# Banded attention and a gated two-layer product on one core: other landing times and due times for the planner that writes the order

## The chip, the cores and the metric

The kernel runs on one core of one Trainium2 chip. The metric is the device time of one execution in microseconds, lower is better. The engines are TensorE (PE, with its weight loads as PEld), VectorE (DVE), ScalarE (ACT), GpSimd (POOL) and SyncE (SP), which issues nearly all transfers in one queue, in order.

## What is computed

```python
scores = scale * np.matmul(q, k.transpose(0, 1, 3, 2))      # 8 batches, 8 heads, 576 x 64
mask = (rel >= 0) & (rel < window)                          # window = 64
scores = np.where(mask, scores, -1000000000.0)
scores = scores - np.max(scores, axis=-1, keepdims=True)
attn = np.exp(scores)
attn = attn / (np.sum(attn, axis=-1, keepdims=True) + 1e-09)
attn_out = np.matmul(attn, v)
x = attn_out.transpose(0, 2, 1, 3).reshape(B * S, H * D)    # 4608 x 512
h = x @ w_in                                                # 512 -> 2048
g = np.where(h >= 1, h, np.where(h <= -1, 0.0, (h + 1) ** 2 / 4))
return g @ w_out                                            # 2048 -> 512
```

All of it is in float32. Each query sees the 64 keys up to itself.

## The kernel before

**Two kinds of work.** The 4608 tokens are 36 attention steps of 128 queries and all 8 heads. Their results feed the two-layer product. The first 1536 tokens are three plain tiles of 512. For each of them PE multiplies 16 pieces of the hidden layer (`ffn_in`, L1118), ScalarE, VectorE and GpSimd make the gate (L1128 to L1150), and PE multiplies by the second matrix (`ffn_out`, L1164). The other 3072 tokens are three supers of 1024 tokens. In a super each matrix product is cut into 2 x 2 blocks and done with seven block products in place of eight, out of sums of blocks. So a super has two halves of 56 products each: L893 (`ffn_product`) and L979 (`out_product`), six matmuls of 128 x 512 to a product, since each float32 operand is split into a high and a low part and three of the four cross terms are taken. The results are added up on VectorE (L908, L998), the gate is on L1128 to L1140, and the operands of the second half are prepared by L957 (sums of blocks), L273 (high part) and L970 (low part). The sums of the blocks of the weights are made once, from the second plain tile on (`add_sums`, L814 to L834), and kept in DRAM (`kept`). From there every product of a super loads its 256 KB (`ring_load`, L873) into one of seven buffers, in turn.

**An attention step.** PE makes the scores (L422, 32 instructions and 64 records of the trace), VectorE adds the mask (L443) and takes the maximum (L452, L453), ScalarE takes the exponential (L464, 16 pieces), VectorE inverts the sum (L475, L476), VectorE or GpSimd normalises (L483), and PE multiplies by V (L534, 16 instructions, 32 records). Before the product with V the weights have to be transposed. Steps 0 to 7 do this on PE or VectorE. Steps from `SOON` = 8 on do it through DRAM: VectorE transposes blocks of 32 x 32 (`att_turn`, L490), SyncE writes the result in two transfers (`att_write`, L501, 192 KB each) to `moved` and reads it back in another shape (`att_read`, L504, 512 KB) into `ptd`, of which there is one buffer for this (called `turned`). The read waits until both writes have landed and until the values of the step before are done; the values wait until the read has landed. I call this way from L490 to L534 the hop. The steps of a super are done in the order 0, 4, 1, 5, 2, 6, 3, 7 during the super before it, and the values become the operands of the next super (L569, L605). Steps 12 to 19 feed the first super, 20 to 27 the second, 28 to 35 the third.

**What sets the order.** A planner (class `Plan`) writes the whole program. Each piece of work has a key, a cost on each engine that may do it, what it needs, the buffers that it takes and gives back, and a lag from the end of its cost to the moment when others may use it. For a transfer the cost is the issue on SyncE and the lag is the landing. The planner goes through time: at each engine, of the pieces that could begin first (within `PATIENCE`), it takes the one with the lowest key. It does this with the constants at the head of the file, and the program then runs in that order, whatever the chip's own times are. An engine that comes to a piece whose input isn't there stands still, with all that is behind it. Keys in turn are due times: `a_keys` for the scores of a step, `B_DUE` for what follows, `R_LEAD` ahead of a product for its ring load, `S_LATE` for the sums of the weights, `OP_LEAD` and `D_LEAD` for the operands, `G_LEAD` for the gates, `BUILD` for the operands of the next super.

Of the kernel before, what the change touches and what calls it, by code (L numbers as in the profile page):

```python
# [40 lines left out]
W_LEAD = 0.57  # L41
W_FIRST = (20.54, -1.96, 1.46, 0.57, -0.16)
W_STEP = 4 / 3
L_LEAD = 2
W_LATE = (3.88, 0.0, -0.24, 7.77, 11.92, 15.5, 19.73)
W_LOAD = 1400
Q_LOAD = 700
# [23 lines left out]
EXP = 1545, 1440  # L71
S_PE = 1230, 1070
B_PE = 2050
B_DUE = 1.0, 2.5, 0.5
B_STEP = 16 / 3
B_FIRST = 3.44
A_END = 1.5
V_PE = 1270
# [1 line left out]
G_LATE = (2.37, 0.0, 0.23, -4.22, 1.33)  # L80
D_LATE = (0.0, 0.0, 2.51, -4.53, 0.66, 1.46)
TURN = 965, 1500
HOP_SP = 600
HOP_LAG = 2300, 2800
PATIENCE = dict(ACT=300, DVE=0, Pool=303, PE=0, SP=0)
BUFS = dict(qt=2, kt=2, vt=4, ps_a=2, sm=2, ptd=3, pt2=1, x=2, u=2, ps_h=2, a=2, gh=2, gl=2, acc=4, o=2, tmp=2)
BUFS.update({n: 1 for n in ("xtmp", "xs0", "xs1", "xs2", "xs3", "xs4", "xs5", "X", "Y")}, raw=4, ring=7, op=5)
# [2 lines left out]
PLAIN = 3  # L90
SUPERS = 3
H_STEP = 18.67
S_LATE = 0
S_PACE = 1.8
O_CHANGE = 3.33, 3.2, 4.7
EARLY_2 = 1.5
A_SUPER = (5, 3.3), (9, 3.6)
A_ORDER = (0, 4, 1, 5, 2, 6, 3, 7)
BUILD = -12, 2
X_SLOTS = 4, 0, 6, 1, 2, 3  # L100
G_FIRST = 8
RING_SLOT = 7
PARTS = (0, 0, 0), (1, 1, 1), (0, 5, 4), (1, 3, 2), (0, 4, 3), (1, 6, 5), (0, 2, 6)
WRITES = (1, None), (2, 1), (0, None), (3, 2), (3, 3), (1, 2), (2, 2)
R_LEAD = 3
R_LOAD = 400
L_DVE = 4, 6, 8
G_LEAD = 0, 0, 0, 0
OP_LEAD = 2.5
D_LEAD = 1.0  # L110


class Plan:
# [10 lines left out]
    def add(self, key, cost, do, after=(), takes=(), gives=(), lag=0, shared=False):  # L124
        self.work.append((key, cost, do, set(after), takes, gives, lag, shared))
        return len(self.work) - 1
# [75 lines left out]
def banded_attention_then_ffn(ctx: ExitStack, tc: tile.TileContext, q, k, v, w, masks, out, out_t, dims):  # L202
# [185 lines left out]
    def load_q(s):  # L388
        qts[s] = t = ld.tile([P, NP, SB], F32, name="qt", bufs=BUFS["qt"])
        nc.sync.dma_start(out=t, in_=q[s])  # L390

    def load_k(s, eng=nc.sync):
        kts[s] = t = ld.tile([P, NP, 3 * QB], F32, name="kt", bufs=BUFS["kt"])
        eng.dma_start(out=t, in_=k[s])
# [255 lines left out]
    def add_step(t, i):  # L650
# [16 lines left out]
            last["r"] = add(lk, dict(ACT=480), lambda e: round_masks())  # L667
        if s == PE_STEPS - 2:
            last["m"] = add(lk + M_LATE, dict(SP=590), lambda e: load_masks(), lag=DMA_LAG)
        xq = add(lk, dict(SP=Q_LOAD), lambda e: load_q(s), takes=["qt"], lag=DMA_LAG)  # L670
        xk = add(lk, dict(SP=K_LOAD), lambda e: load_k(s) if s else None, takes=["kt"], lag=DMA_LAG)
        xv = add(lk + V_LATE, dict(SP=Q_LOAD), lambda e: load_v(s, 0), last["v"], takes=["vt"], lag=DMA_LAG)
        xw = add(lk + V_LATE, dict(SP=Q_LOAD), lambda e: load_v(s, 1), [xv], takes=["vt"], lag=DMA_LAG)
        last["v"] = [xw]
        needs = [xq, xk] + [last["r"]] * masked + last["s"]
        if before:
# [18 lines left out]
        if s < SOON:  # L695
            for h in range(2):
                x = xs
                if not masked:
                    x = add(due + D_LATE[0], dict(DVE=MASKED[near(s)]), lambda e, h=h: att_masked(s, h), [x, last["m"]] if near(s) else [x], gives=[(ps, xs, h)])
                x = add(due + D_LATE[1], dict(DVE=800 if masked else MAXIMUM[near(s)]), lambda e, h=h: att_max(s, h, masked), [x])  # L700
                x = add(
                    due + D_LATE[2], dict(ACT=1375 if masked else EXP[near(s)]), lambda e, h=h: att_exp(s, h, masked), [x],
                    gives=[(ps, xs, h)] * masked,
                )
                x = add(due + D_LATE[3], dict(DVE=420), lambda e, h=h: att_inverse(s, h), [x])
                x = add(due + D_LATE[4], NORM[1], lambda e, h=h: att_normalize(s, h, e), [x], shared=True)
                if not near(s):
                    xt_ = add(
                        key, dict(PE=440), lambda e, h=h: att_transpose_pe(s, h, pt), [x] + turned, takes=[pt],
                        gives=[("sm", xs)] * h,  # L710
                    )
                    turned = [xt_]
                    x = add(
                        due + D_LATE[5], dict(ACT=485, DVE=608), lambda e, h=h: att_transposed(s, h, e), [xt_] + first,
                        takes=["ptd"], gives=[(pt, xt_)],
                    )
                    first = [x]
                    taken.append(x)
                else:
                    x = add(  # L720
                        due, dict(DVE=1890), lambda e, h=h: att_transpose(s, h, 0), [x] + first, takes=["ptd"]
                    )
                    first = [x]
                    taken.append(x)
                    x = add(due, dict(DVE=1890), lambda e, h=h: att_transpose(s, h, 1), [x] + ready, gives=[("sm", xs)] * h)
                ready.append(x)
            gives = [("ptd", taken[0]), ("ptd", taken[1])]
        else:
            due = [key + B_DUE[0], key + B_DUE[0] + B_DUE[2]]
            x = [add(due[h], dict(DVE=MASKED[1]), lambda e, h=h: att_masked(s, h), [xs, last["m"]], gives=[(ps, xs, h)]) for h in range(2)]  # L730
            x = add(due[0], dict(DVE=930), lambda e: att_max(s, BOTH, False), x)
            x = [add(due[h], dict(ACT=EXP[1]), lambda e, h=h: att_exp(s, h, False), [x]) for h in range(2)]
            x = add(due[1], dict(DVE=430), lambda e: att_inverse(s, BOTH), x)
            x = [add(due[1], dict(DVE=870, Pool=1650), lambda e: att_normalize(s, BOTH, e), [x], shared=True)]
            due = key + B_DUE[1]
            if s == SOON:
                z = add(due - 2, dict(Pool=600), lambda e: att_clear(), early_values)
                last["d"] = [add(due - 2, dict(SP=HOP_SP), lambda e, j=j: att_zero(j), [z], lag=HOP_LAG[0]) for j in range(2)]
            x = add(due, dict(DVE=TURN[0]), lambda e: att_turn(s), x, lag=TURN[1])
            x = [add(due, dict(SP=HOP_SP), lambda e, j=j: att_write(s, j), [x, *last["d"]], lag=HOP_LAG[0], gives=[("sm", xs)] * j) for j in range(2)]  # L740
            x = add(due, dict(SP=HOP_SP), lambda e: att_read(), x + last["t"], takes=["pt2"], lag=HOP_LAG[1])
            first = taken = ready = last["d"] = [x]
            gives = [("pt2", taken[0])]
        last["t"] = first
# [93 lines left out]
    def add_sums(l, n):  # L838
        key = step(1) + S_PACE * (n + l * NF // 2) + S_LATE
        ready = [w_ready[2 * n, l], w_ready[2 * n + 1, l], w_ready[NF - 1, 0], w_ready[NF - 1, 1]]  # L840
        xp = add(key, dict(SP=2000), lambda e: sum_pass(l, n), ready, lag=O_LAG_DMA)
        reads, keeps = [xp], [xp]
        for c in range(2):
            k = key + c * S_PACE / 2
            xs = add(
                k, tt(2 * P), lambda e, c=c: sum_whole(l, n, c, 0, e), ready + sum_last,
                takes=["tmp"] if sum_first else ["tmp", "u"], shared=True,
            )
            if not sum_first:
                sum_first.append(xs)  # L850
            x0 = add(k, tt(2 * P), lambda e, c=c: sum_whole(l, n, c, 1, e), [xs], shared=True)
            reads.append(x0)
            sum_last[:] = [xs]
            x = x0
            for j in range(4):
                x = add(k, tt(P), lambda e, c=c, j=j: sum_sums(l, n, c, j, e), [x], shared=True)
            xh = add(k, dict(ACT=90 + .84 * 4 * P), lambda e, c=c: sum_high(l, n, c, e), [x], takes=["o"])
            x = add(k, tt(4 * P), lambda e, c=c: sum_low(l, n, c, e), [xh], shared=True)
            x = add(k, dict(SP=750), lambda e, c=c: sum_keep(l, n, c), [x], lag=O_LAG_DMA, gives=[("tmp", xs), ("o", xh)])
            keeps.append(x)  # L860
        sums_read[l, n], sums_kept[l, n] = reads, keeps

# [12 lines left out]
    def add_ring(l, u, n, j, key):  # L875
        after = [*sums_kept[l, n], *ring_last]
        if l == 0 and u == 0 and n == 0:
            after += freed([RING_SLOT]) + [gates_end[0]] + early_values
        x = add(key - R_LEAD, dict(SP=R_LOAD), lambda e: ring_load(l, u, n, j, x), after, takes=["ring"], lag=DMA_LAG)
        if not ring_last:  # L880
            ring_last.append(x)
        return x
# [127 lines left out]
    def add_outs(u, gates):  # L1010
# [23 lines left out]
        for j in range(7):  # L1034
# [61 lines left out]
            if end:  # L1096
                for m in range(2):
                    gives = []
                    if m:
                        gives = [(("X", box_x) if j == 6 else ("Y", box_y))]  # L1100
                        if j == 5:
                            gives += [("o", o_box, 0), ("o", o_box, 1)]
                    st = add(
                        at, dict(SP=500), lambda e, j=j, m=m, to=to, box=box: out_store(u, to, box, m), [some[m], *([st] if m else [])],
                        lag=O_LAG_DMA, gives=gives,
                    )

    highs = {}
# [283 lines left out]
```

## Time and profile before

| | |
|---|---|
| median of three runs | 905.01 us (902.1 to 910.52) |
| the profiled execution | 911.83 us, its span 909.9 us |
| granted TensorE clock, mean | 0.974 |
| PE busy | 846.9 us, 93% of the span |
| VectorE, ScalarE, GpSimd busy | 712.2, 531.5 and 239.4 us |
| moved by DMA | 213.28 MB, 234 GB/s |

All durations are of the one profiled execution. A row of waits names who waited for whom, the sum, how often and the longest. A row of a group of instructions has its count, then busy time and the mean of one in ns, then the idle time before them and what ended it. In rows of transfers the last number is the median from issue to landing, in us. Names of lines are those of the kernel before; in the changed kernel the same lines stand 8 further down, and from L674 on 10.

### The profile page before, as it was taken

How to read it: one execution, taken by the hardware profiler on the slowest of the kernel's cores; microseconds unless marked ns; L12 is line 12 of the kernel's file. 1: busy time of each engine (PE TensorE's matmuls, PEld its weight loads, DVE VectorE, ACT ScalarE, POOL GpSimd, SP SyncE). 2: the span in 40 equal slices, each digit the busy share in tenths (PEclk: the TensorE clock that was granted, in tenths of full speed). 3: DMA queues.
4: the chain of work that ended last, by engine and by line, in shares of the span. 5: the costliest groups of instructions: out<-in, count | busy, mean ns of one | idle time of the engine just before them, and what ended most of it. 6: DMA issues, size and time to landing. Idle time of an engine off the chain costs nothing.

```text
span 909.9 us, 18124 instructions
## 1 busy us (share of the span) xinstructions
PE 846.9 (93%) x6540; PEld 685.4 (75%) x6540; DVE 712.2 (78%) x1256; ACT 531.5 (58%) x1296; POOL 239.4 (26%) x252
## 2 busy tenths in 40 slices
PE   7899999899998999799988998979988989999998
PEld 6788887678776777678776777868777778888886
DVE  6999995579877774568878974888888965878874
ACT  6999965456654464546665552655764534556442
POOL 1000055447543543111134320222334211110100
PEclk9999999899999999799999999999999999999999
DMA  8991189977987554877877887878876777666775
GB/s 320 418 377 54 40 260 349 369 222 214 274 269 207 161 161 133 271 223 226 259 226 231 277 260 247 246 252 241 284 244 214 230 235 214 194 195 194 191 223 168
DMA packets 149832, 213.28 MB, mean 234 GB/s; under 512 B 11760, under 2 KB 73968, under 8 KB 149744
## 3 DMA queue, kind: packets, MB, share of 16 engines
q1 hardware_dynamic: 149456, 211.22, 74.2%
q8 instruction: 52, 0.85, 0.4%
q10 hardware_dynamic: 288, 0.92, 0.3%
q14 instruction: 36, 0.29, 0.1%
HBM read 162.15 MB, written 49.94 MB: 233 GB/s over the span
## 4 chain that ended last, share of the span: by engine, by line
PE 39%; DMA 16%; DVE 10%; ACT 3%; issue 1%; SPq 1%; POOL 0%; ACTq 0%; POOLq 0%; DVEq 0%
PE acc L979 16%; PE ps_h L893 8%; PE acc L893 8%; DMA ptd<-moved 7%; DMA moved<-sm 5%; PE ps_a L534 3%; PE acc L1164 2%; PE ps_h L1118 2%; DMA kept<-u 1%; DMA wts<-kept 1%; DVE op L970 1%; DVE g L957 1%; ACT sm L464 1%; DVE sm L490 1%; DVE g L1140 1%
## 5 line engine op out<-in xcount | busy, mean ns | idle before, releaser
L979 PE MATMUL acc<-op,wts 128*128 128x512 f32 x576 | 143.5, 401 | 0.0
L1118 PE MATMUL ps_h<-xh,wts 128*128 128x512 f32 (+1 forms) x424 | 134.7, 384 | 7.6 <-DVE a L1140 5.2
L979 PEld LDWEIGHTS acc<-op,wts 128*128 128x128 f32 x576 | 110.9, 194 | 24.2
L273 ACT CAST op<-g 128x512 fp32r<-128x512 f32 x118 | 73.4, 622 | 89.1 <-PE acc L979 68.2
L1164 PE MATMUL acc<-wts,gh 128*128 128x512 f32 x384 | 121.1, 396 | 0.0
L970 DVE TENSOR_TENSOR op<-g,op 128x512 fp32r<-128x512 f32 x105 | 78.0, 744 | 30.0 <-ACT op L273 29.5
L893 PE MATMUL ps_h<-wts 128*128 128x512 f32 x360 | 96.4, 405 | 3.1 <-DMA wts<-kept 3.1
L1118 PEld LDWEIGHTS ps_h<-xh,wts 128*128 128x128 f32 x424 | 79.9, 195 | 25.2 <-DVE a L1140 6.8
L893 PE MATMUL acc<-wts 128*128 128x512 f32 x360 | 94.2, 398 | 0.7 <-DMA wts<-kept 0.7
L464 ACT ACTIVATE sm<-sm,nm 128x96 f32<-128x96 f32 x224 | 80.8, 362 | 19.0 <-DVE nm L453 18.9
L1133 ACT ACTIVATE a<-a 128x512 f32<-128x512 f32 (+1 forms) x139 | 85.7, 617 | 4.3
L1128 ACT ACTIVATE a<-g 128x512 f32<-128x512 f32 x96 | 60.4, 629 | 42.9 <-DVE g L908 38.2
L970 POOL TENSOR_TENSOR op<-g,op 128x512 fp32r<-128x512 f32 x30 | 41.8, 1397 | 159.8 <-DVE op L275 101.3
L893 PEld LDWEIGHTS ps_h<-wts 128*128 128x128 f32 x360 | 69.0, 194 | 18.7 <-issue 3.3
L1164 PEld LDWEIGHTS acc<-wts,gh 128*128 128x128 f32 x384 | 70.7, 189 | 15.3 <-issue 0.3
L1118 PE MATMUL ps_h<-xl,wts 128*128 128x512 f32 (+1 forms) x212 | 80.5, 380 | 0.9 <-DVE xl L547 0.9
L893 PEld LDWEIGHTS acc<-wts 128*128 128x128 f32 x360 | 68.8, 192 | 16.3 <-DMA wts<-kept 1.4
L534 PE MATMUL ps_a<-ptd,vt 128*64 128x64 f32 x992 | 38.1, 233 | 41.2 <-DMA ptd<-moved 26.3
L1164 PE MATMUL acc<-wts,gl 128*128 128x512 f32 x192 | 75.2, 392 | 0.0
L534 PEld LDWEIGHTS ps_a<-ptd,vt 128*64 128x64 f32 x992 | 34.1, 145 | 52.7 <-issue 19.5
L1140 DVE SCALAR_TENSOR_TENSOR g<-a,g 128x512 f32<-128x512 f32 x96 | 67.8, 709 | 3.3 <-ACT a L1133 3.2
L957 POOL TENSOR_TENSOR g<-g 128x512 f32<-128x512 f32 x22 | 31.4, 1430 | 147.1 <-DVE op L970 53.1
(146 smaller groups left out, 1625.4 us busy)
## 6 DMA issues: line engine op xcount, KB each, us to landing
wts<-kept SPq DMA_DIRECT2D x240, 256.0 KB, 3.3
vt<-in_v SPq DMA_DIRECT2D x72, 256.0 KB, 3.7
ptd<-moved SPq DMA_DIRECT2D x28, 512.0 KB, 4.9
kt<-in_k SPq DMA_DIRECT2D x35, 384.0 KB, 5.1
kept<-wts SPq DMA_DIRECT2D x48, 256.0 KB, 4.8
gh<-kept SPq DMA_DIRECT2D x48, 256.0 KB, 3.1
gl<-kept SPq DMA_DIRECT2D x48, 256.0 KB, 3.2
raw<-in_w SPq DMA_DIRECT2D x12, 1023.8 KB, 11.1
```

The lines of the kernel that those rows point to most:

```text
L273: nc.scalar.copy(dst, src)
L464: nc.scalar.activation(t, t, AF.Exp, bias=nm[:, g:g + 1], scale=scale, accum_out=den[:, g:g + 1])
L534: nc.tensor.matmul(ps[half[h], p, n], lhsT=vt[i][:, c:c + D], rhs=w_, start=True, stop=True)
L893: nc.tensor.matmul(ps, lhsT=r[:, part, cp], rhs=x_op(k, xp)[:, cp], start=j in (0, 1, 3, 4) and i == 0 and cp == 0, stop=j in (1, 2, 5, 6) ...
L957: engine[eng].tensor_tensor(out=g[:, out], in0=g[:, a], in1=g[:, b], op=op)
L970: engine[eng].tensor_tensor(out=low, in0=g_of(n)[:, of], in1=high.bitcast(F32), op=ALU.subtract)
L979: nc.tensor.matmul(opened[b][m], lhsT=r[:, part, m], rhs=op[xp], start=j in (0, 1, 3, 4) and i == 0 and n == 0, stop=j in (1, 2, 5, 6) and ...
L1118: nc.tensor.matmul(ps, lhsT=wts[f, 0][:, part, c * P:(c + 1) * P], rhs=x[:, c, r], start=(c == 0 and j == 0), stop=(c == NP - 1 and j == 2),)
L1128: nc.scalar.activation(gs[t, f, r.start][0], phs[t, f, r.start], AF.Relu, bias=0.5, scale=0.5)
L1133: nc.scalar.activation(a, a, AF.Square)
L1140: nc.vector.scalar_tensor_tensor(out=ps if t >= PLAIN else a, in0=a, scalar=1.0, in1=ps, op0=ALU.min, op1=ALU.max)
L1164: nc.tensor.matmul(acc[t, i][:, n], lhsT=g[:, sub], rhs=wts[f, 1][:, part, n], start=(q == 0 and j == 0), stop=(q == NF - 1 and j == 2 and ...
```

## The change

No instruction is added or taken away. The planner gets other numbers. The transfers of the later stage get landing times of their own: for the hop 2900 ns (write) and 4500 ns (read) in place of 2300 and 2800, with an issue cost of 690 and 460 in place of 600; for ring loads, K, Q and V of steps from 8 on 2900, 4500, 3500 and 3100 in place of 1300; for stores of results and of weight sums 3500 in place of 2300, with 1150 in place of 750 to issue a pair of the latter. Loads of V of these steps are due nearly with those of K and Q (`V_LATE_2`), no longer 6.28 later. And the due times and leads of the later stage are other numbers.

```diff
-L_LEAD = 2
+L_LEAD = 2.31
...
-B_DUE = 1.0, 2.5, 0.5
-B_STEP = 16 / 3
+B_DUE = (1.0, 2.34, -0.14)
+B_STEP = 5.21
...
-HOP_SP = 600
-HOP_LAG = 2300, 2800
+HOP_SP = 690, 460
+HOP_LAG = 2900, 4500
+RING_LAG = 2900
+K_LAG = 4500
+Q_LAG = 3500
+V_LAG = 3100
+STORE_LAG = 3500
+SUM_PASS = 1950
+SUM_KEEP = 1150
+V_LATE_2 = 0.15
...
-S_LATE = 0
+S_LATE = 3.55
...
-A_SUPER = (5, 3.3), (9, 3.6)
+A_SUPER = ((5.16, 3.3), (8.9, 3.34))
...
-BUILD = -12, 2
+BUILD = (-14.15, 3.64)
...
-R_LEAD = 3
-R_LOAD = 400
+R_LEAD = 3.76
+R_LOAD = 430
...
-G_LEAD = 0, 0, 0, 0
-OP_LEAD = 2.5
-D_LEAD = 1.0
+G_LEAD = (1.7, 0, 0, 0.54)
+OP_LEAD = 2.0
+D_LEAD = 0.76
...
-        xq = add(lk, dict(SP=Q_LOAD), lambda e: load_q(s), takes=["qt"], lag=DMA_LAG)
-        xk = add(lk, dict(SP=K_LOAD), lambda e: load_k(s) if s else None, takes=["kt"], lag=DMA_LAG)
-        xv = add(lk + V_LATE, dict(SP=Q_LOAD), lambda e: load_v(s, 0), last["v"], takes=["vt"], lag=DMA_LAG)
-        xw = add(lk + V_LATE, dict(SP=Q_LOAD), lambda e: load_v(s, 1), [xv], takes=["vt"], lag=DMA_LAG)
+        late = s >= SOON
+        xq = add(lk, dict(SP=Q_LOAD), lambda e: load_q(s), takes=["qt"], lag=Q_LAG if late else DMA_LAG)
+        xk = add(lk, dict(SP=Q_LOAD if late else K_LOAD), lambda e: load_k(s) if s else None, takes=["kt"], lag=K_LAG if late else DMA_LAG)
+        vk, vl = lk + (V_LATE_2 if late else V_LATE), V_LAG if late else DMA_LAG
+        xv = add(vk, dict(SP=Q_LOAD), lambda e: load_v(s, 0), last["v"], takes=["vt"], lag=vl)
+        xw = add(vk, dict(SP=Q_LOAD), lambda e: load_v(s, 1), [xv], takes=["vt"], lag=vl)
...
-                last["d"] = [add(due - 2, dict(SP=HOP_SP), lambda e, j=j: att_zero(j), [z], lag=HOP_LAG[0]) for j in range(2)]
+                last["d"] = [add(due - 2, dict(SP=HOP_SP[0]), lambda e, j=j: att_zero(j), [z], lag=HOP_LAG[0]) for j in range(2)]
...
-            x = [add(due, dict(SP=HOP_SP), lambda e, j=j: att_write(s, j), [x, *last["d"]], lag=HOP_LAG[0], gives=[("sm", xs)] * j) for j in range(2)]
-            x = add(due, dict(SP=HOP_SP), lambda e: att_read(), x + last["t"], takes=["pt2"], lag=HOP_LAG[1])
+            x = [add(due, dict(SP=HOP_SP[0]), lambda e, j=j: att_write(s, j), [x, *last["d"]], lag=HOP_LAG[0], gives=[("sm", xs)] * j) for j in range(2)]
+            x = add(due, dict(SP=HOP_SP[1]), lambda e: att_read(), x + last["t"], takes=["pt2"], lag=HOP_LAG[1])
...
-        xp = add(key, dict(SP=2000), lambda e: sum_pass(l, n), ready, lag=O_LAG_DMA)
+        xp = add(key, dict(SP=SUM_PASS), lambda e: sum_pass(l, n), ready, lag=O_LAG_DMA)
...
-            x = add(k, dict(SP=750), lambda e, c=c: sum_keep(l, n, c), [x], lag=O_LAG_DMA, gives=[("tmp", xs), ("o", xh)])
+            x = add(k, dict(SP=SUM_KEEP), lambda e, c=c: sum_keep(l, n, c), [x], lag=STORE_LAG, gives=[("tmp", xs), ("o", xh)])
...
-        x = add(key - R_LEAD, dict(SP=R_LOAD), lambda e: ring_load(l, u, n, j, x), after, takes=["ring"], lag=DMA_LAG)
+        x = add(key - R_LEAD, dict(SP=R_LOAD), lambda e: ring_load(l, u, n, j, x), after, takes=["ring"], lag=RING_LAG)
...
-                        lag=O_LAG_DMA, gives=gives,
+                        lag=STORE_LAG, gives=gives,
```

The order is the same until shortly before the values of step 8. From there on all engines have another order. Three places are shown.

SyncE, the hop of step 34 in the second super: two writes (L501), the read (L504), and ring loads (L873). Before:

```order
L873 DMA wts<-kept_106 128x512
L873 DMA wts<-kept_107 128x512
L501 DMA moved<-sm 64x3x256
L873 DMA wts<-kept_108 128x512
L501 DMA moved<-sm 64x3x256
L873 DMA wts<-kept_101 128x512
L873 DMA wts<-kept_102 128x512
L504 DMA ptd<-moved 128x2x512
```

And with the change, where the lines are L509, L512 and L883, and L408 is a load of V:

```order
L509 DMA moved<-sm 64x3x256
L883 DMA wts<-kept_102 128x512
L509 DMA moved<-sm 64x3x256
L883 DMA gh<-kept_103 128x512
L408 DMA vt<-in_v 128x1x512
L883 DMA gl<-kept_104 128x512
L512 DMA ptd<-moved 128x2x512
```

Between the second write and the read stand two ring loads, as before, and now a load of V too.

PE, the values of the same step (the last row), and the products (L979) ahead of them; a product is one row of x6, or five rows where it has its operand in gh and gl; L422 are the scores of step 31. Before:

```order
L979 MATMUL acc<-gh,wts 128x512
L979 MATMUL acc<-gl,wts 128x512
L979 MATMUL acc<-gh,wts 128x512 x2
L979 MATMUL acc<-gl,wts 128x512
L979 MATMUL acc<-gh,wts 128x512
L422 MATMUL ps_a<-kt,qt 32x96 x32
L979 MATMUL acc<-op,gh 128x512 x6
L979 MATMUL acc<-op,gl 128x512 x6
L979 MATMUL acc<-op,wts 128x512 x6
L534 MATMUL ps_a<-ptd,vt 64x64 x16
```

With the change (L989, L430 and L542):

```order
L989 MATMUL acc<-op,gh 128x512 x6
L430 MATMUL ps_a<-kt,qt 32x96 x32
L989 MATMUL acc<-op,gl 128x512 x6
L989 MATMUL acc<-op,wts 128x512 x12
L989 MATMUL acc<-gh,wts 128x512
L989 MATMUL acc<-gl,wts 128x512
L989 MATMUL acc<-gh,wts 128x512 x2
L989 MATMUL acc<-gl,wts 128x512
L989 MATMUL acc<-gh,wts 128x512
L989 MATMUL acc<-op,wts 128x512 x12
L542 MATMUL ps_a<-ptd,vt 64x64 x16
```

Between the scores of step 31 and the values of step 34 stood three products, and now stand six.

PE, the entry to the first super: the last product of the plain tiles (L1164), scores of steps 20 and 24 (L422), and the first products of the super (L893). Before:

```order
L422 MATMUL ps_a<-kt,qt 32x96 x32
L1164 MATMUL acc<-wts,gh 128x512 x2
L1164 MATMUL acc<-wts,gl 128x512
L1164 MATMUL acc<-wts,gh 128x512 x2
L1164 MATMUL acc<-wts,gl 128x512
L422 MATMUL ps_a<-kt,qt 32x96 x32
L893 MATMUL ps_h<-wts 128x512 x6
L893 MATMUL acc<-wts 128x512 x6
```

With the change the rows begin with the values of step 19 (L542), and L430 x64 are the scores of steps 24 and 21:

```order
L542 MATMUL ps_a<-ptd,vt 64x64 x16
L1174 MATMUL acc<-wts,gh 128x512 x2
L1174 MATMUL acc<-wts,gl 128x512
L1174 MATMUL acc<-wts,gh 128x512 x2
L1174 MATMUL acc<-wts,gl 128x512
L1174 MATMUL acc<-wts,gh 128x512 x2
L1174 MATMUL acc<-wts,gl 128x512
L430 MATMUL ps_a<-kt,qt 32x96 x64
L903 MATMUL ps_h<-wts 128x512 x6
L542 MATMUL ps_a<-ptd,vt 64x64 x16
L903 MATMUL acc<-wts 128x512 x6
```

The scores of step 21 have moved ahead of the first product, and the values of step 20 (L542) stand behind the first product, where they stood behind the tenth.

## The prediction

> **What bounds the kernel now.** I read the busy times first, then the kernel cut into stages, then who waited inside each stage, and last the chain of work that ended last.
>
> ```profile
> PE 846.9 (93%) x6540; PEld 685.4 (75%) x6540; DVE 712.2 (78%) x1256; ACT 531.5 (58%) x1296; POOL 239.4 (26%) x252
> PE 39%; DMA 16%; DVE 10%; ACT 3%; issue 1%; SPq 1%; POOL 0%; ACTq 0%; POOLq 0%; DVEq 0%
> ```
>
> TensorE (PE) is busy for 93% of the span, so all that any new order can win is the idle 63 us and what the clock loses. In the chain transfers come second: work on PE alternates with a wait for DMA. The stages show where (columns: sum, busy of PE, PEld, DVE, ACT, POOL, granted clock, DMA share, GB/s):
>
> ```profile
> 165.00:355.00 190.00, 177.34 (x1609) 141.12 (x1609) 140.44 (x261) 105.30 (x306) 91.76 (x104) 0.97 0.73 221
> 355.00:395.00 40.00, 32.88 (x289) 24.97 (x288) 22.83 (x41) 19.37 (x57) 9.58 (x9) 0.83 0.76 240
> 395.00:563.00 168.00, 155.59 (x1203) 125.83 (x1202) 137.85 (x227) 93.28 (x229) 44.83 (x36) 0.97 0.80 246
> 563.00:754.00 191.00, 176.04 (x1442) 142.00 (x1441) 155.30 (x259) 107.45 (x274) 52.67 (x42) 0.98 0.78 242
> 754.00:910.00 156.00, 152.30 (x672) 125.80 (x671) 114.55 (x179) 76.72 (x124) 11.65 (x9) 1.00 0.69 197
> ```
>
> The last stage, the third super, has no attention left and runs at full clock without idle time but for its tail. The first two supers idle 12.4 us (168 - 155.6) and 15.0 us (191 - 176.0) after 395. One group of instructions accounts for nearly all of it:
>
> ```profile
> L534 PE MATMUL ps_a<-ptd,vt 128*64 128x64 f32 x480 | 18.7, 235 | 27.4 <-DMA ptd<-moved 22.3 <-DVE op L275 2.4 <-DVE g L908 1.8
> ```
>
> These are the value products of 15 attention steps (480 matmuls, 32 each) between 395 and 754. PE stood idle for 27.4 us before them, 1.8 us each, for the weights that come back from DRAM (the few us under DVE names are instructions long done; the transfer was last there too). One such hop in the chain, at the end of the first super (start, length, what):
>
> ```profile
> 540.35 0.62 SPq L501
> 541.02 4.90 DMA moved<-sm
> 545.94 5.91 DMA ptd<-moved
> 551.99 1.26 PE ps_a L534 x32
> 553.26 9.83 PE acc L979 x36
> 563.09 1.36 PE ps_h L893 x6
> ```
>
> SyncE issues the write (L501), 4.9 us later it has landed, the read follows at once and takes 5.9 us, and only then does PE go on. The 36 matmuls behind it took 9.83 us. The same 36 took 8.40 us elsewhere, and the granted clock tells why:
>
> ```profile
> 716.97 8.40 PE acc L979 x36
> 460.00:470.00 10.00, 7.30 (x53) 5.84 (x52) 5.50 (x10) 5.29 (x16) 1.79 (x2) 0.83 0.70 239
> 740.00:750.00 10.00, 7.49 (x54) 5.89 (x53) 5.85 (x14) 3.26 (x7) 0.00 (x0) 0.83 0.66 224
> ```
>
> Behind five of the waits (464, 488, 552, 679 and 744 us) the clock is at half for some 3.4 us; 0.83 over 10 us is a loss of 1.7 us each, 8.5 us in all.
>
> **The change, part by part.** No instruction is added or removed. Every term is a wait that another order shortens or makes.
>
> *Value products of the supers (395 to 754).* The planner reckoned with 2300 ns to land the write and 2800 ns for the read. It now reckons with 2900 and 4500. The trace has (between 395 and 754 the count, size and median from issue to landing; in the last row the ns of an issue, shortest, median and longest):
>
> ```profile
> wts<-kept SPq DMA_DIRECT2D x150, 256.0 KB, 3.6
> ptd<-moved SPq DMA_DIRECT2D x14, 512.0 KB, 5.1
> moved<-sm SPq DMA_DIRECT2D x28, 192.0 KB, 4.0
> L873 SPq DMA_DIRECT2D wts<-kept x240: 319/320/1349, 360.7 to 894.1; - x120
> ```
>
> The new figures, with the issue (0.69 and 0.46 us), make 3.6 and 5.0 us against medians of 4.0 and 5.1; the old ones made 2.9 and 3.4. What it does to the order can be counted. SyncE issues in order, and a ring load ahead of the read waits until PE has done the product that held its buffer, seven loads earlier. At ten of the 15 steps that product stood 3 products ahead of the values, at four of them 4; now it is 5 at twelve, 4 at one, and more at the other two. For the last ring load ahead of the second write it was 5 to 7 at all but one and is now 7 or 8, or more. A product is 1.36 us (L893 x6 above). The read's way from that release: load issue 0.32, read 5.1, start of PE and gaps 0.2, some 5.7 us, against 3 x 1.36 = 4.1 us before and 6.8 us now. The write's way: 0.3 + 0.6 + 4.0 + 5.1 + 0.2 = 10.2 us against 6.8 us before and 9.5 us now. So both gain 2 products, 2.7 us, over a mean wait of 1.8 us. What stays is the write's 0.7 us at some steps, nothing at others, and landings longer than the median: I take 0.5 us each, 7.5 us. At the last step of the second super the values move the other way, 17 products behind the scores where it was 20, but the transposition on VectorE (L490) now stands 16 rows behind the masks where it was 28. I count it like the others. **Gain 27.4 - 7.5 = 20 us**, between 5 (if landings lengthen, see the rivals) and 27.
>
> *The clock.* With waits of some 0.5 us I take two thirds of 8.5 us back, **6 us**, between 0 and 8.5. The granted clock fell behind waits of 3.5 us at most:
>
> ```profile
> PE ps_a L534 <- DMA ptd<-moved: 22.3, 11, 3.5
> ```
>
> [...]
>
> *The plain tiles (165 to 355).* PE idles 12.7 us here (190 - 177.3), and 0.97 of 190 us is another 5.7 us of clock.
>
> ```profile
> PE ps_a L534 <- DVE u L821: 5.3, 2, 4.4
> PE ps_h L1118 <- DVE a L1140: 4.3, 3, 3.7
> DVE u L814 <- DMA kept<-u: 15.1, 10, 5.4
> ```
>
> VectorE stands 15.1 us at the head of its queue for the store of the weight sums (L834), whose buffer the next sum (L814) needs, and a gate (L1140) is queued behind it that PE waits for. The planner reckoned with 2.3 us of landing for these stores and 0.75 us of issue, and now with 3.5 and 1.15. These sums also start later (S_LATE 3.55). The eleven hops here get 2.3 us more, as those of the supers. I take half of 18.4, **9 us**, between 0 (SyncE has the same stores to issue either way, and later ones fall among the hops) and 15.
>
> *Entry to the first super (355 to 395).* PE idles 7.1 us, and 0.83 of 40 us is 6.8 us of clock.
>
> ```profile
> PE ps_h L893 <- DMA wts<-kept: 3.1, 1, 3.1
> PE ps_a L534 <- DMA ptd<-moved: 2.9, 1, 2.9
> ```
>
> The first ring load may only go when the last plain product is done. The new order puts the scores of two steps into that gap, where one stood, but the second write of step 20 now stands behind this ring load, and its values come after one product where ten stood. From the last plain product: 0.3 + 0.6 + 4.0 + 5.1 = 10 us to the values, with 3.5 us of work in between (two scores at 1.07, one product), so 6.5 us idle and as much clock lost as now. **0 us**, between -4 and +3.
>
> *Moved at no price.* Loads of V, K and Q change places on SyncE. They are off the path as long as they land before the scores, and no wait for vt, kt or qt of PE stands in these stages. The third super has no waits to win.
>
> Sum: 20 + 6 + 9 + 0 = 35 us. The profiled execution took 911.83 us (span 909.9 and 1.9 around it), so 876.8; the runs shown have a median of 905.01, 0.75% less, and by the same share this is **870 us**.
>
> **The rivals.**
>
> *Landings lengthen with the load, and half of the gain goes.* The same transfers in the plain stage:
>
> ```profile
> ptd<-moved SPq DMA_DIRECT2D x11, 512.0 KB, 4.4
> moved<-sm SPq DMA_DIRECT2D x22, 192.0 KB, 3.0
> ```
>
> At a DMA share of 0.73 write and read make 7.4 us, at 0.79 they make 9.1. The same bytes in 20 us less make a share of some 0.84, by that slope 1.4 us more per hop. Of the 2.7 us half is left: waits of 1.2 us (18 us), a third of the clock term (3), 5 of the plain stage: 9.4 + 3 + 5 = 17, so 888 us. For it speaks the slope; against it, that the step from 0.73 to 0.79 also brings other transfers, not only more. [...]
>
> *The change does not do what it says: VectorE takes the place of the transfers.* It is busy 137.9 of 168 us and 155.3 of 191. In 20 us less that is 0.87 or so, and what is queued on it (transposition, gates, operands) comes late as often as the hops did. PE would wait the 27 us for operands, and only the plain stage gains a little: 900 us. Against it: operands (L970) never show among PE's waits now, and VectorE itself idles 66 us in these stages.
>
> *Slower: a load of V ahead of a write or a read.* These wait longest on SyncE for their buffers (us in total, times, longest):
>
> ```profile
> SPq L873 <- PE acc L979: 79.0, 85, 5.4
> SPq L400 <- PE ps_a L534: 31.3, 12, 5.0
> ```
>
> In the new order such a load stands between a step's first write and its read at seven of the 15 steps, before at two. Should each hold its hop for 8 us, of which 2.7 are covered, that is 7 x 5.3 = 37 us of new waits and 7 x 1.7 = 12 of clock, against 23 us won elsewhere (8/15 of 26, and 9): 26 us more than now, 931 us. It decides from a hold of 5.6 us on (7 x 2.9 + 12 - 23 = 9 us). Against it: the buffer is freed by the values of an earlier step, and so is the buffer that the read itself needs (one `turned`), seven or more products earlier.
>
> **How the numbers follow.** The forecast, 856 to 883, gets 0.62; the longer landings (883 to 898) 0.20; VectorE 0.12; slower 0.06. Of the longer landings I count 0.18 below 896 and put 0.04 of the chance that VectorE leaves some gain there too. The smallest change that a measurement can tell here is 1%, some 9 us. Faster by more: 0.62 + 0.18 + 0.04 = 0.84. Within 1%: 0.10. Slower: 0.06. The range runs from 856 (all 54 us of waits and clock in the first two supers and plain tiles but 5 gone) to 896.
>
> **What would show it.** In the new profile the idle time before the value products of the supers (L542 there) should be near 8 us in place of 27.4, the share of DMA in the chain below a tenth, and the two supers some 13 us shorter each, with a clock of 0.99 after the entry. The wait of VectorE on `kept<-u` should fall by half. The entry keeps its 7 us. Wrong would be: waits of over 1 us left at most value products with landings over 10 us (first rival), idle time before the products (L989, L903 there) in their place (second), or SyncE's waits at the loads of V doubled (third).

## The result and the profile after

The changed kernel takes 866.85 us (median of four runs, 865.92 to 869.91) against 903.56 us before (four runs, 901.72 to 910.52): a ratio of 0.959, interval 0.953 to 0.964. The forecast was 870 us. The profiled execution took 867.29 us.

First the busy times and the chain of the new profile's page:

```profile
PE 829.1 (96%) x6540; PEld 670.8 (78%) x6540; DVE 711.8 (82%) x1254; ACT 530.8 (61%) x1300; POOL 245.9 (28%) x250
PE 67%; DMA 13%; DVE 12%; ACT 3%; issue 2%; SPq 1%; POOL 1%; DVEq 0%; ACTq 0%; POOLq 0%
```

PE has the same 6540 matmuls and is busy 17.8 us less: that is the half clock that is gone (mean granted clock 0.996, before 0.974). VectorE, ScalarE and GpSimd share 2804 instructions as before, with a few of them on another engine. The chain now runs along PE for two thirds of the span; transfers still have 13% of it. The stages, cut where the work is the same as in the windows shown of before (columns: sum, busy of PE, PEld, DVE, ACT, POOL, granted clock, DMA share, GB/s):

```profile
165.00:350.00 185.00, 176.95 (x1711) 140.72 (x1710) 140.60 (x276) 106.93 (x322) 94.51 (x106) 1.00 0.78 236
350.00:390.00 40.00, 34.42 (x284) 27.52 (x284) 28.32 (x48) 22.26 (x62) 9.34 (x9) 0.91 0.90 288
390.00:542.00 152.00, 148.28 (x1132) 120.00 (x1131) 131.88 (x214) 86.31 (x209) 42.26 (x32) 1.00 0.83 261
542.00:716.00 174.00, 172.55 (x1439) 138.72 (x1438) 157.10 (x251) 106.19 (x275) 65.06 (x48) 1.00 0.84 264
716.00:866.00 150.00, 145.77 (x644) 120.40 (x642) 113.65 (x173) 78.75 (x127) 7.77 (x6) 1.00 0.68 196
```

The two supers idle 3.7 us (152 - 148.3) and 1.5 us (174 - 172.6), where it was 12.4 and 15.0, and the granted clock is full there (1.00 in both rows). VectorE is now busy 90% of the second one. The value products of the same 15 steps, between 390 and 716:

```profile
L542 PE MATMUL ps_a<-ptd,vt 128*64 128x64 f32 x480 | 17.3, 225 | 4.8 <-DMA ptd<-moved 4.6
```

4.8 us of idle time before them in place of 27.4. The transfers and SyncE's waits there:

```profile
wts<-kept SPq DMA_DIRECT2D x149, 256.0 KB, 3.9
ptd<-moved SPq DMA_DIRECT2D x14, 512.0 KB, 5.4
moved<-sm SPq DMA_DIRECT2D x26, 192.0 KB, 3.9
```

```profile
SPq L883 <- PE acc L989: 61.3, 79, 2.9
SPq L408 <- PE ps_a L542: 12.8, 12, 1.9
SPq L512 <- DMA moved<-sm: 10.4, 9, 2.7
```

Write and read together land in 9.3 us, against 9.1. SyncE stands half as long ahead of the read for its writes (19.6 us before) and less than half as long at the loads of V (31.3).

By the first product of each super, the profiled span of 909.9 us became 865.5 so (us from the start, or to the next):

| | before | after | change |
|---|---|---|---|
| first product of the first super at | 366.0 | 355.2 | -10.8 |
| first super | 196.9 | 179.5 | -17.4 |
| second super | 190.9 | 174.6 | -16.3 |
| third super and end | 156.1 | 156.2 | +0.1 |

These are 44.4 us; the execution profiled before was a long one (911.83, its median 903.56), and by the medians it is 36.7. One more piece of the 44.4 is chance: in the first 30 us, where both kernels still have the same order on PE, the changed kernel's profile has no half clock, and each of the other 13 profiles has 3.4 us of it or more (before: 3.4 us, a loss of 1.7).

### The profile page after: what moved, and what is told of

Its sections match the earlier page's. It is cut to its first block, busy times and chain, and to the rows that moved or that the text cites. A ratio compares the mean times of both kernels' runs of the same rounds, so it can differ in the third digit from the quotient of the medians.

```text
span 865.5 us, 18101 instructions
## 1 busy us (share of the span) xinstructions
PE 829.1 (96%) x6540; PEld 670.8 (78%) x6540; DVE 711.8 (82%) x1254; ACT 530.8 (61%) x1300; POOL 245.9 (28%) x250
## 4 chain that ended last, share of the span: by engine, by line
PE 67%; DMA 13%; DVE 12%; ACT 3%; issue 2%; SPq 1%; POOL 1%; DVEq 0%; ACTq 0%; POOLq 0%
PE acc L989 16%; PE acc L903 13%; PE ps_h L903 13%; PE acc L1174 10%; PE ps_h L1128 9%; DMA kept<-u 4%; DMA ptd<-moved 3%; PE ps_a L542 2%; DMA raw<-in_w 2%; PE ps_a L430 2%; DVE op L980 2%; DMA moved<-sm 1%; DMA kept<-o 1%; DMA wts<-kept 1%; DVE sm L491 1%
## 5 line engine op out<-in xcount | busy, mean ns | idle before, releaser
L989 PE MATMUL acc<-op,wts 128*128 128x512 f32 x576 | 139.7, 392 | 0.4 <-DVE op L980 0.4
L1128 PE MATMUL ps_h<-xh,wts 128*128 128x512 f32 (+1 forms) x424 | 130.6, 375 | 8.4 <-DVE a L1150 6.7
L989 PEld LDWEIGHTS acc<-op,wts 128*128 128x128 f32 x576 | 107.1, 188 | 24.5 <-DVE op L980 1.3
L281 ACT CAST op<-g 128x512 fp32r<-128x512 f32 x124 | 76.7, 620 | 78.4 <-PE acc L989 43.8
L980 DVE TENSOR_TENSOR op<-g,op 128x512 fp32r<-128x512 f32 x107 | 83.2, 785 | 14.1 <-ACT op L281 13.5
L903 PE MATMUL ps_h<-wts 128*128 128x512 f32 x360 | 93.5, 396 | 0.0
L1143 ACT ACTIVATE a<-a 128x512 f32<-128x512 f32 (+1 forms) x128 | 78.8, 616 | 3.9
L980 POOL TENSOR_TENSOR op<-g,op 128x512 fp32r<-128x512 f32 x28 | 41.7, 1496 | 121.5 <-ACT op L281 104.3
L967 POOL TENSOR_TENSOR g<-g 128x512 f32<-128x512 f32 x26 | 38.1, 1472 | 131.5 <-DVE op L980 57.8
L918 DVE TENSOR_TENSOR g<-g,ps_h 128x512 f32<-128x512 f32 x60 | 41.1, 684 | 20.7 <-PE ps_h L903 20.5
L918 DVE TENSOR_TENSOR g<-g,acc 128x512 f32<-128x512 f32 x60 | 41.0, 683 | 11.1 <-PE acc L903 10.9
## 6 DMA issues: line engine op xcount, KB each, us to landing
raw<-in_w SPq DMA_DIRECT2D x12, 1023.8 KB, 10.5
```

Of the source, the lines that this page charges most:

```text
L281: nc.scalar.copy(dst, src)
L903: nc.tensor.matmul(ps, lhsT=r[:, part, cp], rhs=x_op(k, xp)[:, cp], start=j in (0, 1, 3, 4) and i == 0 and cp == 0, stop=j in (1, 2, 5, 6) ...
L918: nc.vector.tensor_tensor(out=g[:, to], in0=g[:, of], in1=prods[u, n, b], op=ALU.add)
L967: engine[eng].tensor_tensor(out=g[:, out], in0=g[:, a], in1=g[:, b], op=op)
L980: engine[eng].tensor_tensor(out=low, in0=g_of(n)[:, of], in1=high.bitcast(F32), op=ALU.subtract)
L989: nc.tensor.matmul(opened[b][m], lhsT=r[:, part, m], rhs=op[xp], start=j in (0, 1, 3, 4) and i == 0 and n == 0, stop=j in (1, 2, 5, 6) and ...
```

## The experiments

The theory: the planner reckoned the transfers too short, PE came to the value products before the hop's data, and landing times near the measured ones made it do other products first. Rivals: the new due times and leads did it; VectorE stands next behind the hop and takes the gain; and, for the plain tiles, that the weight sums or the hop are at work there. Each ratio is to runs of the kernel before on the same chip, whose medians went from 903.56 to 906.22 us; so rows that lie a few us apart are told apart by the ratios. In the table, "first product" is when the first super's first product begins, "values" the idle time of PE before the value products of the 15 steps, and "clock" what half-clock stretches cost from the last plain product on to the third super, all in us of the profiled execution.

| kernel | median | ratio, interval | first product | first, second super | values | clock |
|---|---|---|---|---|---|---|
| before | 903.56 | | 366.0 | 196.9, 190.9 | 27.4 | 15.4 |
| changed | 866.85 | 0.959 (0.953 to 0.964) | 355.2 | 179.5, 174.6 | 4.8 | 3.4 |
| hop's figures alone | 879.42 | 0.973 (0.966 to 0.980) | 370.7 | 173.1, 175.2 | 4.5 | 1.7 |
| hop's figures undone | 903.94 | 0.998 (0.994 to 1.001) | 367.3 | 191.8, 187.5 | 26.5 | 11.9 |
| due times, no landing times | 902.19 | 0.995 (0.991 to 0.999) | 371.0 | 184.1, 183.5 | 19.3 | 5.1 |
| landing times, old due times | 874.98 | 0.969 (0.961 to 0.977) | 363.9 | 175.6, 176.1 | 6.6 | 1.7 |
| the same, late sums | 869.30 | 0.960 (0.956 to 0.965) | 356.8 | 177.4, 177.5 | 7.1 | 5.1 |
| sums alone | 901.96 | 0.996 (0.993 to 0.998) | 361.6 | 192.0, 195.8 | 29.3 | 15.4 |
| sums undone | 878.85 | 0.970 (0.965 to 0.975) | 368.1 | 175.9, 175.5 | 3.6 | 1.7 |
| before, values from a constant | 867.59 | 0.959 (0.954 to 0.964) | 362.6 | 173.0, 172.2 | 0.0 | 1.7 |
| changed, values from a constant | 867.23 | 0.957 (0.953 to 0.962) | 357.6 | 177.3, 174.4 | 0.0 | 1.7 |
| hop 1000 ns longer each | 881.91 | 0.971 (0.966 to 0.976) | 370.4 | 177.4, 176.2 | 1.9 | 3.4 |
| ring loads together | 863.56 | 0.951 (0.946 to 0.956) | 356.4 | 173.1, 177.3 | 6.0 | 3.4 |
| the same, longer hop in the supers | 866.21 | 0.959 (0.954 to 0.963) | 358.2 | 176.4, 174.5 | 1.6 | 1.7 |

**The hop's figures alone, and undone.** The edit of the first; the second puts the old figures back into the changed kernel.

```diff
-HOP_SP = 600
-HOP_LAG = 2300, 2800
+HOP_SP = 690, 460
+HOP_LAG = 2900, 4500
```

> The kernel before with one edit, the issue cost and landing time of the hop (690 and 460, 2900 and 4500 ns). If the hop's landing times are what the supers gained from, the idle time before the value products of the supers falls from 27.4 us to under 10 and the clock with it, the plain tiles keep their waits: some 878 us (868 to 886). If the due times brought it, 895 us or more and over 20 us of idle time left there.

> The changed kernel with the hop's old figures (600, 2300 and 2800 ns), all else as changed. By the hop: the value products of the supers wait 20 us or more again, 888 us (882 to 898). By the due times: under 876 us and under 10 us of such waits.

Alone, 879.42 us: the idle time before the values falls to 4.5 us and both supers lose some 40 us together. Undone, nothing is left of the gain, 903.94 us. The waits of PE there, between 396 and 747:

```profile
PE ps_a L542 <- DMA ptd<-moved: 19.2, 11, 2.8
PE ps_a L542 <- DVE gl L980: 3.3, 1, 3.3
PE ps_a L542 <- DVE sm L491: 2.6, 1, 2.6
PE ps_a L542 <- DVE op L283: 1.4, 1, 1.4
```

They are the waits of before (26.5 us against 27.4). The new due times and the other new landing times, without the hop's, bring 8 of the 34 us that the supers gain. But the undone kernel was expected at 888 us and lost 16 us more: its plain tiles lost theirs too (first product at 367.3). And with the hop's figures alone the first product comes 4.7 us later. So the plain tiles need more than one of the edits, which the next runs take apart.

**Due times without landing times, and landing times without due times.** In the first all old lags and issue costs, in the second all old due times and leads:

```diff
-HOP_SP = 690, 460
-HOP_LAG = 2900, 4500
-RING_LAG = 2900
-K_LAG = 4500
-Q_LAG = 3500
-V_LAG = 3100
-STORE_LAG = 3500
-SUM_PASS = 1950
-SUM_KEEP = 1150
+HOP_SP = 600, 600
+HOP_LAG = 2300, 2800
+RING_LAG = 1300
+K_LAG = 1300
+Q_LAG = 1300
+V_LAG = 1300
+STORE_LAG = 2300
+SUM_PASS = 2000
+SUM_KEEP = 750
...
```

```diff
-L_LEAD = 2.31
+L_LEAD = 2
...
-B_DUE = (1.0, 2.34, -0.14)
-B_STEP = 5.21
+B_DUE = 1.0, 2.5, 0.5
+B_STEP = 16 / 3
...
-V_LATE_2 = 0.15
+V_LATE_2 = 6.28
...
-S_LATE = 3.55
+S_LATE = 0
...
-A_SUPER = ((5.16, 3.3), (8.9, 3.34))
+A_SUPER = (5, 3.3), (9, 3.6)
...
-BUILD = (-14.15, 3.64)
+BUILD = -12, 2
...
-R_LEAD = 3.76
+R_LEAD = 3
...
-G_LEAD = (1.7, 0, 0, 0.54)
-OP_LEAD = 2.0
-D_LEAD = 0.76
+G_LEAD = 0, 0, 0, 0
+OP_LEAD = 2.5
+D_LEAD = 1.0
```

> The due times, leads and later weight sums of the change with all the old landing times and issue costs. If landing times carry the gain of the supers, these wait 25 us or more before their value products as before: 904 us (896 to 912). If due times do a part by themselves, under 893 us.

> The changed kernel with all its landing times and the old due times and leads. By landing times: 870 us (865 to 880). By due times: 890 us or more.

902.19 and 874.98 us. By the ratios, due times alone are worth 4 to 5 us and landing times alone 28, of 37. Of the 25 us of waits expected for the first run 19.3 are there, in a profiled execution of 896.86 us, one of its shorter ones. In that execution the two supers are 20 us shorter than in the profile before and the first product comes 5 us later; how much of this a median execution has is not known.

**The weight sums: alone, undone, and their start with all landing times.**

```diff
-S_LATE = 0
+S_LATE = 3.55
...
-        xp = add(key, dict(SP=2000), lambda e: sum_pass(l, n), ready, lag=O_LAG_DMA)
+        xp = add(key, dict(SP=1950), lambda e: sum_pass(l, n), ready, lag=O_LAG_DMA)
...
-            x = add(k, dict(SP=750), lambda e, c=c: sum_keep(l, n, c), [x], lag=O_LAG_DMA, gives=[("tmp", xs), ("o", xh)])
+            x = add(k, dict(SP=1150), lambda e, c=c: sum_keep(l, n, c), [x], lag=3500, gives=[("tmp", xs), ("o", xh)])
```

> The kernel before with the figures of the weight sums alone changed (start 3.55 later, 1950 and 1150 ns of issue, 3500 ns to land). If these are what the plain tiles gained from, the first product of the first super comes 8 to 10 us earlier than at 366 us, the supers stay as they are: 896 us (890 to 900). If the plain tiles gain only from the hop's figures and the due times of the loads together, 905 us as before.

> The changed kernel with the old figures of the weight sums (start, issue and landing). If the sums made the gain of the plain tiles, these lose 8 to 10 us and the supers keep theirs: 876 us (872 to 882). If not, 867 us (864 to 871).

> All landing times of the change, the old due times, but for the later start of the weight sums (3.55). If that start is the due time that counts, the plain tiles come from some 360 us to their last product at 351 us: 867 us (863 to 871). If other due times count, 875 us as with the old start.

Undone, the changed kernel loses 10 us by the ratios and by the two profiles, 12.0 by the medians. All of it lies ahead of the first super, whose first product comes 12.8 us later (368.1 against 355.2); the supers keep their gain and win some 3 us more. Alone on the kernel before, the sums win 3.6 us (901.96 against 905.60 on the same chip), less than expected: the first product comes 4.4 us earlier, and the supers have their waits as before. With all landing times and of the due times only the later start, 869.30 us: this start takes 5.7 us off by the medians (7.1 us at the first product), though the intervals overlap. All the other due times together are worth the last 2.4 us, which the intervals don't tell from nothing. So the sums win 4 us at the first product in the kernel before and 13 in the changed one. The hop, short in the plan of the first and long in that of the second, is the likely reason, but the two kernels differ in other figures too, and no run has the old hop and the old sums together with all the rest of the change.

**Value products from a constant: what the hop costs at all.**

```diff
-                    w_ = turned[:, i].rearrange("p (j g n) -> p j g n", j=2, n=SQ)[:, :, h * NP + p] if s >= SOON else pt[h][:, p, n]
+                    w_ = idt[:, :QB].rearrange("p (j n) -> p j n", n=SQ) if s >= SOON else pt[h][:, p, n]
```

> The kernel before, with the value products of the steps from 8 on reading a constant tile in place of the weights that come back from DRAM; all transfers are still made, the attention of these steps is left out of the result. This takes the hop off the path and leaves the order alone. If the waits for the hop are the price, PE loses its 27.4 us before the values of the supers, 8.5 us of clock, and some 10 us in the plain tiles and at the entry: 856 us (850 to 866). If VectorE or the operands behind it are as late as the hops, 880 us or more and new waits before the products.

> The changed kernel with the value products of the steps from 8 on reading a constant tile, all transfers made; the attention of these steps is left out of the result. It shows what the hop still costs. If only the 4.8 us of idle time left before the value products of the supers does: 862 us (859 to 865). If late hops also hold up other work (loads behind them, buffers), 858 us or less.

In the order of before, with the hop off the path, the supers take 173.0 and 172.2 us, without any idle time of PE (393 to 708):

```profile
393.00:708.00 315.00, 315.00 (x2608) 254.80 (x2607) 289.28 (x474) 195.47 (x497) 98.16 (x77) 1.00 0.85 272
```

So the hop was all that PE waited for there. The two supers are 42.5 us shorter, the half clock behind the waits included; some 3 us of this are of another wait, that for the first ring load, behind which the clock was at half for 10.2 us before and for 3.4 here. VectorE, at 92%, had not been in the way. The plain tiles kept most of their idle time (10.5 us of 12.7). The total of 867.59 us is above the 856 expected: the two profiles differ by 45.9 us, as was reckoned from the profile before, but that was a long execution, and the medians differ by 37.6. The changed kernel without the hop is no faster than with it (867.23 us), where 862 us was expected. Its waits between 388 and 709 tell why:

```profile
PE acc L989 <- DVE op L980: 2.7, 5, 1.3
PE acc L989 <- POOL op L980: 1.2, 1, 1.2
PE acc L989 <- DVE gl L980: 0.8, 2, 0.6
```

Where the values no longer wait, the operands do (L980 is L970 of before). In that order the last 4.8 us at the values cover 4.7 us of other waits, for work of VectorE and GpSimd.

**A hop that is reckoned too long, and the same in the supers alone.**

```diff
-HOP_LAG = 2900, 4500
+HOP_LAG = 3900, 5500
```

> The changed kernel with a hop that is reckoned 1000 ns longer for the write and for the read than measured (3900, 5500). If slack costs nothing, the idle time left before the value products goes and the time stays, since operands are late next: 867 us (863 to 871). If values that come later hold up buffers and the operands of the next super, 872 us or more.

881.91 us, 15 us more than the changed kernel by the medians and by the traces, 11 by the ratios, against the expectation. The supers are hardly touched (177.4 and 176.2). The plain tiles lose it, with PE waiting for gates, between 165 and 366:

```profile
PE ps_h L1128 <- DVE a L1150: 13.0, 4, 4.9
```

and VectorE, in the same window, at the head of its queue:

```profile
DVE a L1150 <- ACT a L1143: 21.0, 11, 4.8
DVE u L839 <- ACT o L281: 17.7, 9, 4.2
DVE u L824 <- DMA kept<-u: 9.9, 5, 5.8
```

In the changed kernel PE's wait for gates was 3.9 us up to 350, and the first two of these waits of VectorE were 8.2 and 6.1 us, the third 11.9. So gates now come later, and the sums (L839) that stand on the same engine wait longer for ScalarE; that the one makes the other is read from these rows and not tested. To be sure that the place is the plain tiles, the last run lengthened the hop from step 20 on only:

```diff
-            x = add(due, dict(SP=HOP_SP[1]), lambda e: att_read(), x + last["t"], takes=["pt2"], lag=HOP_LAG[1])
+            x = add(due, dict(SP=HOP_SP[1]), lambda e: att_read(), x + last["t"], takes=["pt2"], lag=HOP_LAG[1] + 1000 * (s >= 20))
```

and the same for the write, on the kernel with the ring loads together (below).

> The kernel of the run before with the ring loads together, and the hop reckoned 1000 ns longer for the write and the read from step 20 on only. If the longer hop cost its time in the plain tiles alone, their last product stays at some 352 us, the 6 us of idle time before the value products of the supers fall by half or more, and the time is 860 to 864 us. If it costs as much in the supers (values later, operands later), 867 us or more.

The first super's first product is at 358.2 us (370.4 with the hop longer everywhere), so the loss was in the plain tiles. The values wait 1.6 us in place of 6.0, and nothing is won by it: 866.21 us, above the 860 to 864 expected, and a ratio of 0.959 against 0.951, with intervals that overlap. The waits between 389 and 709:

```profile
PE acc L987 <- ACT op L281: 2.1, 1, 2.1
PE acc L987 <- DVE op L978: 2.0, 5, 0.7
PE ps_a L542 <- DMA ptd<-moved: 1.6, 3, 0.8
PE acc L987 <- DVE gl L978: 0.2, 1, 0.2
```

They add up to 5.9 us; in the kernel with the ring loads together they were 5.9 us too, all at the values. The second rival is right about this last piece: behind the hop stand the operands, most of them VectorE's.

**Ring loads together at the entry.** In the plan every later ring load needed the first one to have landed, so a longer landing time moved the second one back. This kernel gives the later loads what the first one needs:

```diff
+        if not ring_last:
+            ring_last.extend(freed([RING_SLOT]) + [gates_end[0]] + early_values)
         after = [*sums_kept[l, n], *ring_last]
-        if l == 0 and u == 0 and n == 0:
-            after += freed([RING_SLOT]) + [gates_end[0]] + early_values
         x = add(key - R_LEAD, dict(SP=R_LOAD), lambda e: ring_load(l, u, n, j, x), after, takes=["ring"], lag=RING_LAG)
-        if not ring_last:
-            ring_last.append(x)
```

> The changed kernel in which the second and later ring loads need what the first one needs, not the first one itself, so that seven of them stand together ahead of the read of step 20 at the entry to the first super. If the wait of the second product for its ring load (3.4 us, and 3.4 us of clock) is what the entry costs, 863 us (860 to 866). If the values of step 20, now later, only move the wait, 867 us.

863.56 us, 3.3 less than the changed kernel by the medians, as expected, though the intervals (0.946 to 0.956, 0.953 to 0.964) overlap. The first super is some 6 us shorter and the second some 3 longer. SyncE's queue of the changed kernel at the entry, and PE's waits between 351 and 391:

```profile
343.75 1.23 SPq L509 DMA_DIRECT2D moved<-sm  x2
...
350.79 0.43 SPq L883 DMA_DIRECT2D wts<-kept  x1
351.32 0.40 SPq L512 DMA_DIRECT2D ptd<-moved  x1
...
353.38 0.82 SPq L1202 DMA_DIRECT2D out<-o  x2
354.25 3.28 SPq L883 DMA_DIRECT2D wts<-kept  x4
```

```profile
PE acc L903 <- DMA wts<-kept: 3.4, 1, 3.4
PE ps_a L430 <- DVE sm L451: 1.8, 1, 1.8
PE ps_a L542 <- issue: 0.2, 1, 0.2
```

The second ring load goes 3.5 us after the first, behind the read of step 20, loads of Q and K, and stores, and the second product waits 3.4 us for it. With the loads together the same window has

```profile
PE ps_a L430 <- DVE sm L451: 1.8, 1, 1.8
```

alone. By its median it is the fastest kernel of this study.

## Why the prediction was right, step by step

**The sum: too small, and the time close in part by luck.** In the profiles 44.4 us were won, and the sum had 35. The forecast of 870 us came within 3 us of 866.85 all the same, since the execution profiled before was 8.3 us above its median; which of the terms are larger in it than in a median execution is not known.

**What bounds: right.** Waits for the hop were the loss of the supers. The kernel before with values from a constant shows it directly.

**Value products, 20 us: the mechanism right, a little too small.** 22.6 us were won (27.4 - 4.8; I had 7.5 left). The count of products between the release of a ring buffer and the values, times 1.36 us, against the way of the read and of the write, was enough to tell that most of these waits would go. Undoing the figures of the hop brought the waits back (26.5 us). The share of DMA in the chain, which I had expected below a tenth, fell only from 16 to 13%: the hop's part went from 12 to 4%, but other stores and loads came into the chain.

**The clock, 6 us: too small.** All of the 8.5 us came back in the supers. The waits that are left, up to 1.4 us, cost no clock (1.00 in both supers). That waits of some 0.5 us would still cost a third of it was an estimate. In the kernel before it did not go by the length of a wait alone whether clock was lost, see the last section.

**The plain tiles, 9 us: right in size, the way half wrong.** Idle time fell from 12.7 to 8.1 us and the clock's loss from 5.1 to nothing, 9.7 us. I had named first VectorE's wait for the stores of the sums, which should halve, with the gates queued behind it, and second the hops. The wait for the stores hardly fell, 11.9 us in place of 15.1:

```profile
DVE u L824 <- DMA kept<-u: 11.9, 6, 2.9
```

Nor did PE's wait for gates, 4.3 us before. What went is its wait at the value products. Before, the 5.3 us under `DVE u L821` and these rows stood there:

```profile
PE ps_a L534 <- DVE wts L605: 1.2, 1, 1.2
PE ps_a L534 <- DMA ptd<-moved: 1.0, 1, 1.0
PE ps_a L534 <- DVE sm L443: 0.8, 1, 0.8
```

Four of these five waits, 7.5 us, ended some 0.1 us after a read of the hop had landed (the longest: landed at 286.84, values at 286.93), so here too the hop was waited for, and the names `u L821` and `wts L605` are of work long done. After, PE's longest waits in these tiles are

```profile
PE ps_h L1128 <- DVE a L1150: 3.9, 5, 1.7
PE acc L1174 <- POOL gl L1160: 1.4, 2, 0.8
```

and no value product waits over 0.2 us. With the hop's figures alone these waits are gone as well, but PE waits for gates instead:

```profile
PE ps_h L1118 <- DVE a L1140: 11.4, 6, 3.8
```

That this costs the tiles 5 us, unless the sums change too, was not in the sum at all. Neither edit carries the gain by itself: without the sums' figures the changed kernel's first product comes 12.8 us later, without the hop's 12.0.

**The entry, 0 us: this step failed, by 5 us.** I had put the second write of step 20 behind the first ring load, and so its values 6.5 us late. It is the read that stands there; both writes went at 343.75 us, and the values waited 0.2 us. Instead the second product waited for its ring load. Idle time fell from 7.1 to 5.6 us and the clock's loss from 6.8 to 3.4.

**The rivals.** Landings that lengthen with the load: the DMA share rose from 0.79 to 0.84 as reckoned, but the hop grew by 0.2 us (9.1 to 9.3), not 1.4. What made it longer in the supers than in the plain tiles stays open. The changed kernel's plain tiles, at a share of 0.78, have 7.9 us for write and read, where the supers before had 9.1 at 0.79:

```profile
ptd<-moved SPq DMA_DIRECT2D x11, 512.0 KB, 4.8
moved<-sm SPq DMA_DIRECT2D x24, 192.0 KB, 3.1
```

So the share alone does not set it. VectorE in place of the transfers: not for the 27 us, as the constant shows, but for the last 5. Loads of V ahead of writes: SyncE's waits at them fell, from 31.3 to 12.8 us.

## What to carry to other kernels

A planner's order is as good as its transfer times: take them from the trace, by kind of transfer and stage, and count in the order how much work stands between the release that an in-order queue waits for and the instruction that needs the data. Reckoning longer "to be safe" is not free, since it reorders everything else: 1 us more on each transfer of the hop cost 11 to 15 us here, in a stage where the hop wasn't late. And when a wait is down to the size of the next one behind it, removing it wins nothing (here 867.23 us without the hop, 866.85 with it); taking the data from a constant shows in one run where that point is.

## What the runs showed of the hardware

Whether TensorE's clock fell did not go by the length of one wait alone. In the kernel before a wait of 3.1 us at 609 us cost no clock, and one of 2.4 us at 676 us did (columns as in the stages; the clock is 1.00 in the first stretch and 0.86 in the second, a loss of 1.7 us):

```profile
608.00:628.00 20.00, 16.90 (x161) 13.53 (x160) 14.77 (x26) 9.04 (x27) 3.71 (x4) 1.00 0.75 237
672.00:684.00 12.00, 9.65 (x63) 7.82 (x62) 8.53 (x17) 6.85 (x25) 3.67 (x3) 0.86 0.68 235
```

In that profile the half-clock stretches inside the span are 3.41 us long, one 6.83 and one 10.24, and they begin at 13.58, 139.87, 177.42, 286.65, 365.15, 389.05, 464.14, 488.03, 552.89, 679.18 and 744.03 us: times that lie a multiple of 3.41 us apart. I laid this grid through the 14 traces, from 45 us on, and took PE's idle share in each full-clock cell. Leaving out the last 2 us of each trace, 61 cells are followed by half clock: they were idle for 46 to 100%. 3263 are not: none was idle for over 57%. Between 46% and 57% both happened. The wait at 609 us lay across two cells (from 607.50 us 43% and from 610.91 us 48% idle), the one at 676 us within one (from 675.77 us, 69%), and the half clock began at 679.18 us, where that cell ends. So of these two waits the shorter one cost 1.7 us more and the longer one nothing. That two kernels with the same idle time can differ by as much is an estimate from these two waits; no pair of runs was made to show it.
